# A new instruction order for routed attention and its gated convolution: centroids first, the first pair's argmax split by head, fewer idle products

## The chip, the core and the metric

The kernel runs on one core of a Trainium2 chip. A core has five engines with a queue each, worked off in order: TensorE (PE, matmuls and transposes), VectorE (DVE), ScalarE (ACT, activation functions and copies), GpSimd (POOL) and SyncE (SP, which only issues transfers here). They meet through semaphores. The metric is the device time of one execution in microseconds (us); lower is better.

## The reference

Two stages follow one another. First, attention in which a query sees only the keys of its own cluster; a head's cluster of a row is the argmax of its similarity with 16 centroids:

```python
q_n = q / (norm(q) + 1e-6); k_n = ...; c_n = centroids / (norm(centroids) + 1e-6)
q_assign = argmax(einsum('bhsd,hcd->bhsc', q_n, c_n)); k_assign = argmax(...)
mask = q_assign[:, :, :, None] == k_assign[:, :, None, :]
scores = where(mask, q @ k.T / sqrt(D), -1e9)
x = softmax(scores) @ v            # batch 4, heads 8, sequence 768, head size 64
```

Then, on the heads side by side (4 x 768 x 512), a product with a long convolution, done by a Fourier transform over the sequence:

```python
proj = x @ w_proj; x1, x2, x3 = thirds of proj
x2_conv = irfft(rfft(x2, axis=1) * rfft(filter_fft, axis=0), axis=1)
out = (x1 * x2_conv * x3) @ w_out
```

## The kernel before

`build` first describes the whole program as some 1,950 steps (`op`), each with the engines that may run it, what it reads and writes, and a function that issues its instructions. The list `ORDER` then fixes everything by hand: one number for each step, five times its place in the description plus the engine's number (PE 0, ACT 1, DVE 2, POOL 3, SP 4). `arrange` follows this list; it sets the order within each engine's queue and the PSUM bank that a step gets. A step that the list hands to another engine is computed there, with that engine's own instruction.

The work is cut into eight groups of four heads (`n` = 0 to 7, two for each batch), each of two pairs of heads (`pr`). For a pair, six blocks of 128 keys are taken in turn: TensorE makes scores in three banks (line 158; 156 where the array is used whole), ScalarE takes their exponentials into one of five buffers `p` (lines 690, 693), VectorE adds the buffers up for the denominators (713, 717; GpSimd does some of 713), and TensorE multiplies them with v (704). In between stand the routing of the next group and the convolution of finished batches (`hyena`), whose sums, products and gates on lines 852 to 964 VectorE and GpSimd share as the list says.

The mask is part of the scores' product. Beside the 64 rows of a head, `aug` has 16 rows that hold, for a key, a one at its cluster, and for a query, 0 at its cluster and a large negative number elsewhere.

The start is a path of its own. `warm` lets TensorE run `WARM` idle products (line 1101) on a tile of ones. `centroids` loads the centroids, normalizes them (square, sum, root on ScalarE, one step of Newton on lines 324 to 329), turns them and writes them to `cbd` (337, 338). `routing(0)` turns q and k of the first group in pieces of three 128-row blocks (602), each with an idle product `awake` ahead of it, and copies them to `qkP` (246, 248). `first_masks(pr)` makes the similarities (502), turns them (511) and finds the argmax in five VectorE steps (518 to 525): the largest of 16, who equals it, times a falling ramp `revc`, the largest again, who equals that. For the first pair the resulting words are turned (535) and copied to the mask rows of `aug` (`put`: 546 and 248, one for each head and for q and k); for the second they go through a transfer. `angles` meanwhile makes the arguments of the sines (357 to 375) for three tables m = 0, 1, 2, and `constants` ramps, zero fills (1072, 1074) and an identity.

Of the kernel before, what the change touches and what calls it, by code (L numbers as in the profile page):

```python
# [15 lines left out]
BF16 = mybir.dt.bfloat16  # L16
# [212 lines left out]
def build(T):  # L229
# [261 lines left out]
    def first_masks(pr):  # L491
# [35 lines left out]
        if pr == 0:  # L527
            for j in (1, 0):
                h2 = Bank("head")

                def rows(e, j=j, h2=h2):
                    o = ap(h2).bitcast(BF16)
                    for t in range(NT):
                        for hp in range(2):
                            T.nc.tensor.transpose(o[64 - 64 * hp:80 - 64 * hp, ts(t, 128)], oh()[:, at(t) + 2 * j + hp], T.identb)
# [755 lines left out]
```

## Time and profile before

| | |
|---|---|
| time, median of 3 | 348.03 us (347.56 to 348.55) |
| profiled execution | 348.1 us, of which the span from first to last instruction 346.3 us |
| granted TensorE clock, mean | 0.997 |
| busy: TensorE, VectorE, ScalarE, GpSimd | 336.8, 327.6, 274.2, 135.1 us |
| instructions: VectorE, ScalarE, GpSimd | 438, 509, 161 |
| first exponential starts | 16.52 us |

In a row of the profile stand the line, the engine, the operation, the tiles written and read, their shape, the count, the busy time and the mean of one. A matmul's end is modelled from the pipeline, so TensorE's busy time is rougher than VectorE's. In a row of the timeline, the first number is the start in us from the span's start, the second how long it took.

### The profile page before, as it was taken

The numbers are of one execution on the slowest core, as the hardware profiler recorded it, in microseconds if no ns is written. First come the engines' busy times: TensorE is split into PE (matmuls) and PEld (weight loads), VectorE is DVE, ScalarE is ACT, GpSimd is POOL, SyncE is SP. The second block draws the span as 40 slices with busy tenths as digits, with TensorE's granted clock in tenths as the row PEclk, the third lists the DMA queues.
The fourth block names the chain that finished last, engine by engine and source line by source line (L and its number), as shares of the span: only waits on it lengthen the run. The fifth ranks groups of instructions, "written<-read, shape, count | busy, mean of one in ns | idle before, by whom it ended". The sixth has DMA issues, their size and how long they took to land.

```text
span 346.3 us, 8366 instructions
## 1 busy us (share of the span) xinstructions
PE 336.8 (97%) x3164; PEld 194.7 (56%) x3165; DVE 327.6 (95%) x438; ACT 274.2 (79%) x509; POOL 135.1 (39%) x161
## 2 busy tenths in 40 slices
PE   8899999999999999999999999999999999999994
PEld 4464465454455556655665656676455555576672
DVE  6899999999999999999999999999999999989992
ACT  7999999999799989887898797697998655524442
POOL 6423407004115447234702686126501161336740
PEclk9999999999999999999999999999999999999998
DMA  8979986775799997798969776998748321500124
GB/s 184 195 150 208 181 168 125 123 152 122 161 160 157 141 169 89 153 117 185 142 124 167 132 126 150 195 135 128 164 103 142 72 25 43 173 5 2 74 110 184
DMA packets 132052, 46.19 MB, mean 133 GB/s; under 512 B 119192, under 2 KB 124140, under 8 KB 132012
## 3 DMA queue, kind: packets, MB, share of 16 engines
q1 hardware_dynamic: 127884, 35.79, 49.9%
q0 software_dynamic: 2752, 8.98, 18.7%
q10 hardware_dynamic: 1376, 0.89, 0.8%
q8 instruction: 25, 0.41, 0.5%
q14 instruction: 15, 0.12, 0.1%
HBM read 31.59 MB, written 7.40 MB: 113 GB/s over the span
## 4 chain that ended last, share of the span: by engine, by line
PE 81%; ACT 8%; DVE 8%; issue 1%; ACTq 0%; DVEq 0%
PE bank L158 38%; PE pair L704 32%; PE bank L838 5%; PE bank L622 3%; DVE acc L717 2%; ACT aug L246 1%; PE bank L733 1%; DVE tm L868 1%; PE bank L455 1%; ACT p L693 1%; ACT qkP L246 1%; ACT sim L648 1%; DVE ohB L637 1%; DVE oh L635 1%; DVE mx L633 1%
## 5 line engine op out<-in xcount | busy, mean ns | idle before, releaser
L704 PE MATMUL pair<-p,vraw 128*64 128x385 f32 x768 | 142.1, 487 | 0.0
L693 ACT ACTIVATE p<-bank 128x512 f32<-128x512 f32 x192 | 108.6, 606 | 22.5 <-PE bank L158 19.8
L717 DVE TENSOR_TENSOR acc<-p,acc 128x1536 f32<-128x1536 f32 x64 | 112.9, 1765 | 2.6 <-ACT p L693 0.2
L158 PE MATMUL bank<-aug 128*64 128x512 bf16 (+1 forms) x738 | 83.7, 327 | 0.3 <-ACT p L693 0.2
L704 PEld LDWEIGHTS pair<-p,vraw 128*64 128x64 f32 x768 | 57.9, 136 | 42.6 <-issue 33.7
L158 PEld LDWEIGHTS <-aug 128*64 128x64 bf16 (+1 forms) x738 | 45.0, 109 | 36.7 <-issue 25.3
L754 POOL DMA_DIRECT2D acc<-acc x30 | 23.9, 796 | 98.4 <-DVE acc L717 61.4
L690 ACT ACTIVATE p<-bank 128x512 f32<-128x512 f32 x96 | 57.1, 609 | 5.4 <-PE bank L158 4.3
L158 PE MATMUL bank<-xT,wpj 128*64 128x384 bf16 x504 | 49.4, 326 | 0.0
L158 PEld LDWEIGHTS <-wpj 128*64 128x64 bf16 x504 | 30.9, 110 | 14.4 <-issue 4.6
L246 ACT CAST aug<-qkP 64x768 bf16<-64x768 f32 x46 | 37.7, 829 | 0.8
L713 POOL TENSOR_TENSOR acc<-p,p 128x1536 f32<-128x1536 f32 x7 | 24.3, 3474 | 29.6 <-DVE acc L717 27.8
L158 PEld LDWEIGHTS <-y 128*64 128x64 bf16 x488 | 24.6, 110 | 12.7 <-issue 4.1
L868 DVE TENSOR_TENSOR tm<-bank,hm 128x512 f32<-128x512 f32 x44 | 27.9, 681 | 1.1 <-PE bank L455 0.5
L158 PE MATMUL bank<-wout,y 128*64 128x512 bf16 (+1 forms) x200 | 23.9, 371 | 0.2 <-DVE y L964 0.2
L579 DVE STREAM_TRANSPOSE qkP<-qkraw 128x768 f32<-128x768 f32 x26 | 24.0, 953 | 0.0
L838 PE MATMUL bank<-wpj,xT 128*64 128x512 bf16 x192 | 22.8, 379 | 0.4 <-ACT tm L246 0.4
L872 POOL TENSOR_TENSOR y<-tm 128x512 bf16<-128x512 f32 x15 | 19.0, 1274 | 10.6 <-DVE tm L868 8.2
L964 POOL TENSOR_TENSOR y<-yy,x 128x768 bf16<-128x768 f32 x9 | 16.4, 1827 | 15.1 <-DVE acc L717 7.1
L246 ACT COPY x<-bank 128x384 f32<-128x384 f32 x27 | 13.1, 484 | 11.4 <-PE bank L158 10.6
L246 ACT COPY ob<-bank 128x512 f32<-128x512 f32 x22 | 12.8, 589 | 11.1 <-PE bank L158 9.4
L248 POOL CAST aug<-qkP 64x768 bf16<-64x768 f32 x15 | 12.5, 840 | 17.7 <-DVE acc L717 7.4
(175 smaller groups left out, 415.0 us busy)
## 6 DMA issues: line engine op xcount, KB each, us to landing
rb<-dr SPq DMA_DIRECT2D x30, 192.0 KB, 3.5
qkraw<-in_k_dram SPq DMA_DIRECT2D x55, 96.0 KB, 3.2
qkraw<-in_q_dram SPq DMA_DIRECT2D x55, 96.0 KB, 3.2
vraw<-in_v_dram SPq DMA_DIRECT2D x52, 96.0 KB, 3.2
out_dram<-ob SPq DMA_DIRECT2D x9, 512.0 KB, 3.2
acc<-acc POOLq DMA_DIRECT2D x10, 384.0 KB, 5.2
acc<-acc POOLq DMA_DIRECT2D x10, 192.0 KB, 4.0
y<-in_moe_filter_fft_dram SPq DMA_DIRECT2D x4, 384.0 KB, 4.9
```

The lines of the kernel that those rows point to most:

```text
L158: T.nc.tensor.matmul(out[64 * i:64 * i + 64], lhsT[:, 64 * i:64 * i + 64], rhs, start=start, stop=stop)
L246: T.nc.scalar.copy(out, in_)
L579: op(("DVE", .96), lambda e, s=s, z=z, j=j: V().transpose(T.qkP[z // 2][:, ts(j, S)], T.qkraw[s][:].rearrange("p t h d -> p (t h d)") if j ...
L690: T.nc.scalar.activation(o, ap(h).rearrange("p (a b) -> p a b", a=2), Act.Exp, scale=0.125)
L693: T.nc.scalar.activation(flat(s)[:, lo:lo + 512], ap(h), Act.Exp, scale=0.125)
L704: T.nc.tensor.matmul(o[64 * hp:64 * hp + 64, ch, :385], T.vraw[vs][:, hp, sk * D:(sk + 1) * D], T.p[slots[sk]][:, hp, 384 * ch:384 * ch + ...
L713: alu(e).tensor_tensor(T.acc[os], T.p[slots[0]][:, :, :S], T.p[slots[1]][:, :, :S], op=Alu.add)
L717: T.nc.vector.tensor_tensor(T.acc[os], T.p[slots[sk]][:, :, :S], T.acc[os], op=Alu.add)
L754: op(("POOL", .8), lambda e, rows=rows: T.nc.gpsimd.dma_start(flat_()[:rows], flat_()[rows:2 * rows], accum_op=Alu.add), te, r=[], w=AK, b ...
L838: T.nc.tensor.matmul(ap(h)[64 * i:64 * i + 64], T.xT[xs][:, kt, c:c + 64], T.wpj[:, kt, DM:2 * DM], start=kt == 0, stop=kt == ND - 1)
L868: op(("DVE", .68), lambda e, i=i, cs=cs, r=r, h=h: T.nc.vector.tensor_tensor(T.tm[r][:, cs], ap(h), hmrow(i, (0, 2, 2, 3)[2 * r + cs]), op ...
L872: op({"POOL": 1.5, "DVE": .68}, lambda e, i=i, r=r: alu(e).tensor_tensor(T.y[:, i, r], T.tm[r][:, 0], T.tm[r][:, 1], op=Alu.add if r else ...
```

## The change

Four things change in the description, and the list is a new one throughout.

- `WARM` falls from 10 to 8, and the four transposes of the first pair (z = 0, 1) lose their idle product.
- The first pair's five argmax steps are done for each of the two heads apart, on every second of 24 columns; so are the transposes of its words. Each head's q and k have a bank of their own.
- The order's start is set so that the centroids' load is the first that SyncE issues, and their sum of squares the first real work of VectorE; the sine tables' arguments for m = 0 are made after the first masks.
- Every step has a new place, and about 65 steps have another engine.

```diff
-WARM = 10
+WARM = 8
...
-        if pr == 0:
-            for j in (1, 0):
...
+        for hp in range(2) if pr == 0 else (None,):
+            N = 24 if hp is None else 12
+            k = ((pr,) if hp is None else (pr, hp))
+            part = (lambda x: x) if hp is None else (lambda x, hp=hp: x[:, hp::2])
...
+            op(("DVE", D_[0]), lambda e, part=part: V().tensor_reduce(part(mx()), part(sv()), axis=AX, op=Alu.max), dd + .5, r=[h], w=[("mx", *k)])
...
+            for j in (1, 0) if pr == 0 else ():
                 h2 = Bank("head")
...
                     for t in range(NT):
-                        for hp in range(2):
-                            T.nc.tensor.transpose(o[64 - 64 * hp:80 - 64 * hp, ts(t, 128)], oh()[:, at(t) + 2 * j + hp], T.identb)
+                        T.nc.tensor.transpose(o[64 - 64 * hp:80 - 64 * hp, ts(t, 128)], oh()[:, at(t) + 2 * j + hp], T.identb)
...
-                    if n == 0:
+                    if n == 0 and z > 1:
                         awake(h)
...
 ORDER = [
-    2, 179, 106, 28, 5, 171, 23, 32, 154, 161, 184, 18, 48, 169, 13, 98, 159, 37, 62, 51, 206, 66, 58, 267, 189, 272, 277, 149, 43, 112, 236, 117,
+    2, 109, 23, 161, 5, 176, 169, 13, 37, 18, 184, 149, 103, 154, 51, 112, 206, 48, 117, 267, 58, 174, 122, 237, 272, 126, 159, 81, 132, 199, 98, 86,
```

Behind the hunks on line 518 the numbers of the lines grow by 6 or 7 (602 becomes 608, 964 becomes 970).

Two places of VectorE's queue show what the list did. The first is the first pair's argmax up to the second pair's first step, before (`bank_65` holds the first pair's turned similarities, `bank_154` the second's; `aug_97` and `aug_98` are the first pair's two heads):

```order
L518 TENSOR_REDUCE mx<-bank_65 128x24
L519 TENSOR_TENSOR oh<-bank_65,mx 128x384
L521 TENSOR_TENSOR oh<-oh,revc 128x384
L523 TENSOR_REDUCE m_87<-oh 128x24
L525 TENSOR_TENSOR oh<-oh,m_87 128x384
L248 CAST aug_98<-qkP_113 64x768
L546 TENSOR_SCALAR aug_97<-bank_68 16x768
L248 COPY aug_97<-bank_153 16x768
L546 TENSOR_SCALAR aug_98<-bank_68 16x768
L518 TENSOR_REDUCE mx<-bank_154 128x24
```

and the same place now, from the first head's second step on (its first, of line 525, stands ahead of these):

```order
L526 TENSOR_TENSOR oh<-bank_63,mx 128x12x16
L525 TENSOR_REDUCE mx<-bank_63 128x12
L528 TENSOR_TENSOR oh<-oh,revc 128x12x16
L530 TENSOR_REDUCE m_87<-oh 128x12
L532 TENSOR_TENSOR oh<-oh,m_87 128x12x16
L526 TENSOR_TENSOR oh<-bank_63,mx 128x12x16
L528 TENSOR_TENSOR oh<-oh,revc 128x12x16
L530 TENSOR_REDUCE m_87<-oh 128x12
L532 TENSOR_TENSOR oh<-oh,m_87 128x12x16
L248 COPY aug_97<-bank_67 16x768
L551 TENSOR_SCALAR aug_97<-bank_153 16x768
L248 COPY aug_98<-bank_154 16x768
```

Five steps became ten, the two heads' steps follow each other, the cast of `aug_98` left this place, and the mask copies stand behind both heads' steps.

The second place is VectorE's queue behind the last sum of exponentials (`yy` is the folded convolution, `y_135` its product with the gates, `xT` the attention's output, `x_141` the gates). Before:

```order
L717 TENSOR_TENSOR acc_118<-p_103,acc_118 128x1536
L248 COPY od<-bank_64 128x384
L919 TENSOR_TENSOR x_141<-bank_68,x_141 128x2x192
L946 TENSOR_TENSOR sd<-bank_67,od 128x384 x2
L956 TENSOR_TENSOR yy<-sd 128x2x192
L785 RECIPROCAL dn<-bank_65 128x12
L964 TENSOR_TENSOR y_135<-yy,x_141 128x768
```

and now:

```order
L723 TENSOR_TENSOR acc_118<-p_103,acc_118 128x1536
L962 TENSOR_TENSOR yy<-sd 128x2x192
L773 RECIPROCAL dn<-dn 128x12
L962 TENSOR_TENSOR yy<-sd 128x2x192
L970 TENSOR_TENSOR y_135<-yy,x_140 128x768
L810 SCALAR_TENSOR_TENSOR xT_132<-osb_120,rb 128x2x192 x2
L952 TENSOR_TENSOR sd<-bank_65,od 128x384 x2
L962 TENSOR_TENSOR yy<-sd 128x2x192
L925 TENSOR_TENSOR x_141<-bank_66,x_141 128x2x192
L791 RECIPROCAL dn<-bank_68 128x12
L970 TENSOR_TENSOR y_135<-yy,x_141 128x768
```

Two folds and a gate that GpSimd had in the old list stand in VectorE's queue here, ahead of the weighing of the attention's output (`xT`).

More of the change, by code (lines that the diff above doesn't have):

```diff
@@ L516, in first_masks @@
         mx, m2 = lambda: T.mx[:, pr], lambda: T.m2[:, pr]
-        bc = lambda a: a.unsqueeze(2).to_broadcast([128, 24, NC])
-        op(("DVE", .55), lambda e: V().tensor_reduce(mx(), sv(), axis=AX, op=Alu.max), due + .5, r=[h], w=[("mx", pr)])
-        op(("DVE", .55), lambda e: V().tensor_tensor(oh(), sv(), bc(mx()), op=Alu.is_equal), due + .6,
-           r=[h, ("mx", pr)], w=[("oh", pr)], free=[h])
-        op(("DVE", .35), lambda e: V().tensor_tensor(oh(), oh(), T.revc[:].unsqueeze(1).to_broadcast([128, 24, NC]),
-                                                     op=Alu.mult), due + .7, r=["revc"], w=[("oh", pr)], lock=True)
@@ L523, in first_masks @@
-        op(("DVE", .55), lambda e: V().tensor_reduce(m2(), oh(), axis=AX, op=Alu.max), due + .8, r=[("oh", pr)],
-           w=[("m2", pr)])
-        op(("DVE", .55), lambda e: V().tensor_tensor(oh(), oh(), bc(m2()), op=Alu.is_equal), due + .9,
-           r=[("m2", pr)], w=[("oh", pr)], lock=True)
-        if pr == 0:
-            for j in (1, 0):
+        put_ = []
+        for hp in range(2) if pr == 0 else (None,):
+            N = 24 if hp is None else 12
+            k = ((pr,) if hp is None else (pr, hp))
+            part = (lambda x: x) if hp is None else (lambda x, hp=hp: x[:, hp::2])
+            bc = lambda a, N=N: a.unsqueeze(2).to_broadcast([128, N, NC])
+            D_ = (.55, .36) if hp is None else (.36, .26)
+            dd = due + .5 * (hp or 0)
+            op(("DVE", D_[0]), lambda e, part=part: V().tensor_reduce(part(mx()), part(sv()), axis=AX, op=Alu.max), dd + .5, r=[h], w=[("mx", *k)])
+            op(("DVE", D_[0]), lambda e, part=part, bc=bc: V().tensor_tensor(part(oh()), part(sv()), bc(part(mx())), op=Alu.is_equal), dd + .6,
+               r=[h, ("mx", *k)], w=[("oh", *k)], free=[h])
+            op(("DVE", D_[1]), lambda e, part=part, N=N: V().tensor_tensor(
+                part(oh()), part(oh()), T.revc[:].unsqueeze(1).to_broadcast([128, N, NC]), op=Alu.mult), dd + .7, r=["revc"], w=[("oh", *k)], lock=True)
+            op(("DVE", D_[0]), lambda e, part=part: V().tensor_reduce(part(m2()), part(oh()), axis=AX, op=Alu.max), dd + .8, r=[("oh", *k)],
+               w=[("m2", *k)])
+            op(("DVE", D_[0]), lambda e, part=part, bc=bc: V().tensor_tensor(part(oh()), part(oh()), bc(part(m2())), op=Alu.is_equal), dd + .9,
+               r=[("m2", *k)], w=[("oh", *k)], lock=True)
+            for j in (1, 0) if pr == 0 else ():
@@ L529, in first_masks, with rows @@
                 h2 = Bank("head")
-                def rows(e, j=j, h2=h2):
+                def rows(e, j=j, hp=hp, h2=h2):
                     o = ap(h2).bitcast(BF16)
                     for t in range(NT):
-                        for hp in range(2):
-                            T.nc.tensor.transpose(o[64 - 64 * hp:80 - 64 * hp, ts(t, 128)], oh()[:, at(t) + 2 * j + hp], T.identb)
-                op(("PE", .35), rows, due + 1.0 + .1 * (1 - j), r=[("oh", 0), "identb"], w=[h2], alloc=h2, kind="sim")
@@ L537, in first_masks @@
-                for hp in range(2):
-                    def put(e, j=j, hp=hp, h2=h2):
-                        rs = slice(64 - 64 * hp, 80 - 64 * hp)
-                        o, x = T.augs[0][hp][j][rs], ap(h2).bitcast(BF16)[rs, :S]
-                        if j:
-                            copy(e, o, x)
-                        elif e == "ACT":
-                            T.nc.scalar.activation(o, x, Act.Copy, scale=BIG, bias=-BIG)
-                        else:
-                            V().tensor_scalar(o, x, BIG, -BIG, op0=Alu.mult, op1=Alu.add)
-                    got = op({"ACT": .8, "DVE": .55}, put, due + 1.2 + .3 * hp, r=[h2, ("zero", 0, j)],
-                             w=[("augm", 0, hp, j)], free=[h2])
@@ L549, in first_masks, with put @@
-            return [got]
+                        T.nc.tensor.transpose(o[64 - 64 * hp:80 - 64 * hp, ts(t, 128)], oh()[:, at(t) + 2 * j + hp], T.identb)
+                op(("PE", .21), rows, dd + 1.0 + .1 * (1 - j), r=[("oh", *k), "identb"], w=[h2], alloc=h2, kind="sim")
+                def put(e, j=j, hp=hp, h2=h2):
+                    rs = slice(64 - 64 * hp, 80 - 64 * hp)
+                    o, x = T.augs[0][hp][j][rs], ap(h2).bitcast(BF16)[rs, :S]
+                    if j:
+                        copy(e, o, x)
+                    elif e == "ACT":
+                        T.nc.scalar.activation(o, x, Act.Copy, scale=BIG, bias=-BIG)
+                    else:
+                        V().tensor_scalar(o, x, BIG, -BIG, op0=Alu.mult, op1=Alu.add)
@@ L550, in first_masks @@
+                put_ = [op({"ACT": .8, "DVE": .55}, put, dd + 1.2 + .3 * hp, r=[h2, ("zero", 0, j)],
+                           w=[("augm", 0, hp, j)], free=[h2])]
+        if pr == 0:
+            return put_
         h2 = Bank("head")
@@ L596, in routing, with tr @@
                 h = Bank(cls)
-                def tr(e, s=s, ch=ch, j=j, h=h):
-                    if n == 0:
+                def tr(e, s=s, ch=ch, z=z, h=h):
+                    if n == 0 and z > 1:
                         awake(h)
@@ L602, in tr @@
                         T.nc.tensor.transpose(ap(h)[:, ts(t, 128)], raw(s, 3 * ch + t), T.ident)
-                op(("PE", .58 if n == 0 else .36), tr, due, r=[("qkraw", s, x, c) for x in range(2) for c in (range(4) if n else (ch, ch + 2))] + [("raw", s, x, y) for x in range(2) for y in range(2)] + ["ident"] + ["cold", "warmed", ("wpj", 0)] * (n == 0), w=[h], alloc=h)
+                op(("PE", .58 if n == 0 and z > 1 else .36), tr, due, r=[("qkraw", s, x, c) for x in range(2) for c in (range(4) if n else (ch, ch + 2))] + [("raw", s, x, y) for x in range(2) for y in range(2)] + ["ident"] + ["cold", "warmed", ("wpj", 0)] * (n == 0), w=[h], alloc=h)
                 op(EV384 if n != 1 else {"ACT": .48}, lambda e, z=z, ch=ch, h=h: copy(e, T.qkT[z][:, ch], ap(h)[:, :384]),
@@ L628, in routing @@
                r=[h], w=[("sim", ch, 0), ("sim", ch, 1)], free=[h])
-        both = lambda x: [(x, 0), (x, 1)]
+        both = lambda x: [(x, 0, 0), (x, 0, 1), (x, 1)]
         sims = lambda: T.sim[:].rearrange("p a (m c) -> p (a m) c", c=NC)
```

158 rows, old and new, of the table ORDER are left out of this document.

## The prediction

> **What bounds the kernel now.** I read the page first, then busy time by stretch, then the waits of VectorE, then single rows. The page says that two engines are full, not one:
>
> ```profile
> span 346.3 us, 8366 instructions
> ...
> PE 336.8 (97%) x3164; PEld 194.7 (56%) x3165; DVE 327.6 (95%) x438; ACT 274.2 (79%) x509; POOL 135.1 (39%) x161
> ...
> PE   8899999999999999999999999999999999999994
> ...
> DVE  6899999999999999999999999999999999989992
> ```
>
> By stretch (columns: length, then busy us and instructions of PE, PEld, DVE, ACT, POOL), from the first scores to the last gate:
>
> ```profile
> core 0: us, PE busy (x) PEld busy (x) DVE busy (x) ACT busy (x) POOL busy (x), PEclk, DMA share, GB/s
> ...
> 20.00:300.00 280.00, 278.52 (x2534) 157.75 (x2532) 273.95 (x329) 237.31 (x436) 104.79 (x101) 1.00 0.76 136
> 300.00:339.50 39.50, 39.29 (x499) 26.36 (x495) 37.13 (x68) 17.50 (x35) 20.50 (x17) 1.00 0.20 71
> ```
>
> VectorE is idle 6.05 + 2.37 = 8.42 us of 319.5. What it waited for in that stretch, nine rows in all, of which the first three and the last stand here:
>
> ```profile
> DVE x L919 <- PE bank L158: 1.1, 2, 0.8
> DVE dn L785 <- ACT x L246: 0.8, 1, 0.8
> DVE tm L868 <- PE bank L455: 0.5, 1, 0.5
> ...
> DVE tm L868 <- PE bank L158: 0.2, 1, 0.2
> ```
>
> The other five are 0.2 each, so the nine come to 3.6 us at most. The 4.8 us left over, spread over 397 instructions, are 12 ns each: gaps between instructions that wait for nothing. So VectorE works without a real pause from about 11 us to the last gate. TensorE's 278.5 of 280 looks as full, but the page says that the ends of matmuls are modelled; VectorE's rows carry no such caveat. Since the last instruction ahead of the final products is a VectorE gate (338.93, below), I take VectorE's work to set the end: what the new order adds to its queue comes out at the end, less what real waits can swallow.
>
> **The head: idle products and centroids.** TensorE runs idle products until the first transposes; ScalarE and VectorE then feed the first masks:
>
> ```profile
> 1.12 4.87 PE L1101 MATMUL bank<-wpj 128*128 128x512 bf16 x11 [1.12 <-DVE wpj L1105]
> 5.79 0.79 PE L602 MATMUL bank<-ident,qkraw 128*128 128x128 f32 x3
> ...
> 6.63 0.49 PE L602 MATMUL bank<-ident,qkraw 128*128 128x128 f32 x3
> ...
> 9.22 0.85 PE L502 MATMUL bank<-qkP,cbd 128*32 128x384 f32 x8 [0.36 <-ACT ob L368]
> ```
> ```profile
> 4.29 0.83 ACT L1074 ACTIVATE aug<-ident 64x768 bf16<-64x768 f32 x1
> ...
> 8.62 0.53 ACT L368 ACTIVATE ob<-tm 128x384 f32<-128x384 f32 x1
> 9.18 0.62 ACT L375 ACTIVATE wout<-ob,half_pi 128x384 bf16<-128x384 f32 x1
> 9.70 0.46 ACT L246 COPY qkP<-bank 128x384 f32<-128x384 f32 x1
> ```
>
> Eleven idle products take 4.87 us (0.43 from one to the next); now eight stand ahead of the first transposes, which could begin 3 x 0.43 = 1.3 us sooner. But the similarities at 9.22 need more: the centroid table, which VectorE writes behind the centroids' chain and two copies of turned q and k, and ScalarE's copies. The chain now stands ahead of most angle work, yet it waits for the centroids' load, which changes queues (from ScalarE's first issue to SyncE's first; the loads behind it keep their places, since one k load goes the other way). And ScalarE's copy of the similarities, before behind a sine and a copy (0.62 + 0.46), now stands behind an absolute value and a zero fill (0.53 + 0.83), 0.28 more; against it ScalarE issues one load less at the start. I price the start of the first argmax at no change, with 0.3 us either way, from that 0.28.
>
> [...] A start that stays cold is a rival below.
>
> **The first masks.** VectorE's rows of before, and one short row of the centroids for size:
>
> ```profile
> 4.67 0.22 DVE L319 TENSOR_REDUCE ss<-sd 128x1 f32<-128x64 f32 x1
> ...
> 11.32 0.56 DVE L518 TENSOR_REDUCE mx<-bank 128x24 f32<-128x384 f32 x1 [0.86 <-PE bank L511]
> ...
> 12.57 0.36 DVE L521 TENSOR_TENSOR oh<-oh,revc 128x384 bf16<-128x384 bf16 x1
> ...
> 13.55 0.56 DVE L525 TENSOR_TENSOR oh<-oh,m 128x384 bf16<-128x384 bf16 x1
> 14.14 0.56 DVE L248 CAST aug<-qkP 64x768 bf16<-64x768 f32 x1
> 14.73 0.56 DVE L546 TENSOR_SCALAR aug<-bank 16x768 bf16<-16x768 bf16 x1
> ...
> 16.26 0.54 DVE L518 TENSOR_REDUCE mx<-bank 128x24 f32<-128x384 f32 x1
> 16.73 0.54 DVE L248 COPY aug<-bank 16x768 bf16<-16x768 bf16 x1
> 17.29 0.56 DVE L519 TENSOR_TENSOR oh<-bank,mx 128x384 bf16<-128x384 f32 x1
> ...
> 18.86 0.56 DVE L525 TENSOR_TENSOR oh<-oh,m 128x384 bf16<-128x384 bf16 x1
> ```
>
> Five instructions of 384 elements become ten of 192. Between 0.22 us at 64 elements and 0.56 at 384, 192 elements come to 0.36; the 0.36 row (two-byte operands) to some 0.25. Eight of 0.36 and two of 0.25 are 3.4 us, with ten gaps of 0.03 3.7, where the five took 2.8 (11.32 to 14.14). If a half took no fixed time the ten would be 2.8, if as long as a whole 5.6: -0.9 to +1.9 around the value taken. The cast at 14.14 moves ahead of the chain (-0.6). The four mask copies (14.73 to 17.29 with one reduction, so 2.0 without) all stand behind both heads' words in the new queue, so the first head's earlier words buy no earlier mask: the first copy starts 3.7 us after the chain's start, before 3.4. The second pair's five whole steps follow as they did. Sum for the point where the second pair's words are ready: +0.9 - 0.6 = **+0.3 us**; TensorE's queue holds that pair's transposes ahead of the first weighted sums in both orders, so nothing passes it there.
>
> **The rest of VectorE's queue.** The new order also hands whole steps to other engines. Net, between that point and the last gate, at these groups' mean ns:
>
> ```profile
> L964 DVE TENSOR_TENSOR y<-yy,x 128x768 bf16<-128x768 f32 x3 | 2.9, 950 | 0.1
> ...
> L857 DVE TENSOR_TENSOR uv<-tm,tm 128x512 bf16<-128x512 f32 x12 | 7.9, 695 | 0.0
> ...
> L872 DVE TENSOR_TENSOR y<-tm 128x512 bf16<-128x512 f32 x9 | 6.1, 691 | 0.1
> ...
> L433 DVE TENSOR_SCALAR tm<-bank,hw 128x512 f32<-128x512 f32 x2 | 1.4, 744 | 0.0
> ...
> L363 DVE SCALAR_TENSOR_TENSOR tm<-x,s0t,ob 128x384 f32<-128x384 f32 x3 | 1.9, 644 | 0.1
> ...
> L361 DVE TENSOR_SCALAR ob<-ob 128x384 f32<-128x384 f32 x3 | 1.2, 397 | 0.1
> ```
> ```profile
> 338.93 0.56 DVE L964 TENSOR_TENSOR y<-sim,qkP 128x384 bf16<-128x384 f32 x1
> ```
>
> Two more whole gates (+1.90) and one half gate less (-0.56); two more sums of spectra (+1.39); one more product difference (+0.69); two scalings to ScalarE (-1.49); the two angle steps of m = 0, before ahead of the masks, now behind (0.40 + 0.64 = +1.04); one more cast (+0.56); small ones (a mask row step, copies, two tiny constants) about +0.3. Sum **+3.8 us**. GpSimd, which gives most of these up, was busy 104.8 of 280 us, so what it sheds buys nothing; nor does ScalarE's relief of five casts, with 43 us free in that stretch. GpSimd now makes the index ramps before all else, which moves its other constants by a few of its rows and delays no engine that was waiting for them here. TensorE has the same products in the long middle; the six idle products less are at the start. The tables that ScalarE loads are as many as before, five.
>
> **The sum.** The profiled execution took 348.1 us (span 346.3), beside a median of 348.03, so no correction is needed. 348.1 + 0.0 + 0.3 + 3.8 = 352.2 if nothing is swallowed. The waits of 3.6 us, most of them behind 300 us, where about 2 of the 3.8 are added (both gates among them), can swallow between nothing and all. I take half, 1.8: **350.4 us**, 0.7% slower. Its own range: all swallowed and the start 0.3 early, 348.3; nothing swallowed and 0.3 late, 352.5.
>
> **Rivals.**
> *TensorE is the bound.* Then VectorE's extra work disappears in its gaps, and the end follows TensorE's start: the first transposes 1.3 us early, less the 0.3 of the mask chain, gives 348.1 - 1.0 = 347.1. For it: 278.5 of 280. Against it: VectorE's 12 ns gaps, and that four other steps stand between the transposes and the masks. It decides if the added steps fit in gaps. Chance 0.2.
> *Everything swallowed.* The start does not move and the 3.8 us find their waits: 348.1 + 0.3 = 348.4, no change that shows (about 0.3%, 1.0 us, is what a measurement of this kernel can tell from none). For it: the order may have been laid so that each added step falls in a pause. Against it: the pauses come to 3.6 us and are single. Chance 0.17.
> *A cold start.* With eight products and no idle ones between the first pair's transposes, the array could stay slow until the argmax: two transpose groups 0.3 longer each, the similarities 0.85 and the next transposes 0.5 longer, 2.0 on the way to the masks: 352.4. For it: 0.79 against 0.49. [...] Chance 0.08.
>
> **How the numbers follow.** The forecast has 0.55. Faster by over 0.3% is the first rival, 0.2; within, the second, 0.17; slower, forecast and cold start, 0.63. The range reaches from the first rival's 347.1 to 352.5.
>
> **What would show it.** Right: VectorE's busy sum up by 4 to 5 us with waits below 2 us between 20 us and the last gate; first mask copy no earlier than 14.7; last gate near 341. Wrong: the last gate before 339 with VectorE busier; half-size steps far from 0.36; the first reduction before 11.0; or idle time on TensorE in the middle with VectorE waiting too, which would be a wait that I did not see (SyncE's queue, where loads for the second group now stand ahead of the first V load).

## The result, and the profile after

The changed kernel takes **358.66 us** (median of 4, 356.46 to 359.43) where the kernel before takes 348.02 on the same chip: 1.0288 times as long, 95% interval 1.0266 to 1.0310. That is 10.6 us slower. The forecast was 350.4 with a range up to 352.5: the sign was right, the size was not.

The page of the changed kernel (profiled execution 358.81 us) shows at once where to look. In its second part each digit is a slice of 8.9 us. TensorE has a dent in slices 5 and 6, from 36 to 54 us, VectorE in slices 6 and 7, and the granted clock in slice 6:

```profile
span 357.1 us, 8344 instructions
...
PE 340.8 (95%) x3149; PEld 191.2 (54%) x3149; DVE 330.4 (93%) x449; ACT 271.1 (76%) x505; POOL 136.5 (38%) x159
...
PE   7999669999999999999999999999999999999994
...
DVE  5789947999999999999989999999999999999984
...
PEclk9999969999999999999999999999999999999998
```

By stretches of 20 us (length, then busy us and instructions of PE, PEld, DVE, ACT, POOL, then the clock), before and after:

```profile
40.00:60.00 20.00, 19.84 (x178) 11.33 (x176) 19.90 (x22) 19.53 (x36) 7.69 (x9) 1.00 0.82 158
```
```profile
40.00:60.00 20.00, 14.41 (x104) 7.14 (x100) 13.05 (x14) 12.53 (x23) 10.70 (x16) 0.83 0.60 104
```

TensorE, VectorE and ScalarE all lose 5 to 7 us there; only GpSimd is busier. Its timeline in the changed kernel, with TensorE's and VectorE's of the same microseconds:

```profile
39.77 0.82 POOL L248 CAST aug<-qkP 64x768 bf16<-64x768 f32 x1 [6.50 <-PE bank L158]
40.54 0.53 POOL L1096 DMA_DIRECT2D wpj<-in_moe_w_proj_dram  x1
41.10 6.22 POOL L407 TENSOR_SCALAR hw<-ph 128x3 f32<-128x3 f32 x5
...
47.36 0.10 POOL L381 MEMSET fw<- 128x2 bf16 x1
47.39 0.09 POOL L381 MEMSET wout<- 128x1 bf16 x1
```
```profile
41.58 0.41 PE L158 MATMUL bank<-aug 80*64 80x512 bf16 x2
47.51 1.07 PE L158 MATMUL bank<-uv,fw 128*64 128x512 bf16 x4 [5.52 <-POOL wout L381]
```
```profile
40.91 1.74 DVE L719 TENSOR_TENSOR acc<-p,p 128x1536 f32<-128x1536 f32 x1
42.69 0.56 DVE L656 TENSOR_SCALAR sim<-bank 64x384 bf16<-64x384 f32 x1
43.17 1.74 DVE L723 TENSOR_TENSOR acc<-p,acc 128x1536 f32<-128x1536 f32 x1
44.83 0.55 DVE L248 CAST aug<-qkP 64x768 bf16<-64x768 f32 x1
45.30 1.75 DVE L723 TENSOR_TENSOR acc<-p,acc 128x1536 f32<-128x1536 f32 x1
```

Line 407 is five scalings of three columns each: the factors `hw` of the filter's spectrum. They took 6.22 us. Behind them in GpSimd's queue stand two writes of constants (line 381) into the sine tables, and TensorE's first products with these tables waited 5.52 us for them. In the kernel before, the same five scalings took 1.42 us, and the constants were there before TensorE asked:

```profile
35.69 1.42 POOL L407 TENSOR_SCALAR hw<-ph 128x3 f32<-128x3 f32 x5
...
39.91 0.10 POOL L381 MEMSET fw<- 128x2 bf16 x1 [2.18 <-ACT fw L375]
```

In cuts of 0.2 us, for line 407 alone, a cut with two instructions is one in which the rows of two scalings meet or overlap:

```profile
42.60:42.80 0.20, 0.20 (x2) 1.00 0.82 147
42.80:43.00 0.20, 0.20 (x2) 1.00 1.32 221
...
44.20:44.40 0.20, 0.20 (x1) 1.00 1.05 190
...
44.60:44.80 0.20, 0.20 (x1) 0.50 1.15 184
44.80:45.00 0.20, 0.20 (x2) 0.50 0.80 124
...
45.40:45.60 0.20, 0.20 (x2) 0.50 0.05 8
45.60:45.80 0.20, 0.20 (x1) 0.50 0.00 0
...
47.00:47.20 0.20, 0.20 (x2) 0.50 0.00 0
```

VectorE's three sums end at 40.91 + 1.74 = 42.65, 43.17 + 1.74 = 44.91 and 45.30 + 1.75 = 47.05. Each time the next scaling starts within 0.1 us of that end, in finer cuts at 42.74, 44.97 and 47.11. Of the five, two took 0.22 us and three were held:

```profile
L407 POOL TENSOR_SCALAR hw<-ph x5: 216/1657/2485, 41.1 to 47.1; 128x3 f32<-128x3 f32 x5
```

The first (1.66 us) and the fourth (2.16) end within 0.1 us of a sum's end. The third, the longest with 2.49, does not: its row goes from 42.93, a little ahead of the second sum, to 45.42, past that sum and to the end of VectorE's cast (44.83 + 0.55). What held it behind the sum, no run takes apart. The fourth column of these cuts is TensorE's granted clock: it falls to half at 44.6, 2.6 us after TensorE's last product (41.58 + 0.41). When TensorE goes on at 47.51, a set of four products takes 1.07 us. (`fw` and `wout` are the sine tables, `acc` the sums of the exponentials.)

The start is late too. The nine first transposes took 2.15 us, the similarities 1.38 where they took 0.85 before, and the first argmax began at 11.89, where it was 11.32 before:

```profile
5.71 2.15 PE L608 MATMUL bank<-ident,qkraw 128*128 128x128 f32 x9 [0.99 <-DMA qkraw<-in_q_dram]
...
9.33 1.38 PE L502 MATMUL bank<-qkP,cbd 128*32 128x384 f32 x8 [0.61 <-DVE tm L363]
```
```profile
11.89 0.36 DVE L525 TENSOR_REDUCE mx<-bank 128x12 f32<-128x192 f32 x1
...
14.84 0.36 DVE L532 TENSOR_TENSOR oh<-oh,m 128x192 bf16<-128x192 bf16 x1
15.23 0.56 DVE L248 COPY aug<-bank 16x768 bf16<-16x768 bf16 x1
```

### The profile page after: what moved, and what is told of

The parts are those of the page before. It is cut to its first block, busy times and chain, and to the rows that moved or that the text cites. A ratio compares the mean times of both kernels' runs of the same rounds, so it can differ in the third digit from the quotient of the medians.

```text
span 357.1 us, 8344 instructions
## 1 busy us (share of the span) xinstructions
PE 340.8 (95%) x3149; PEld 191.2 (54%) x3149; DVE 330.4 (93%) x449; ACT 271.1 (76%) x505; POOL 136.5 (38%) x159
## 4 chain that ended last, share of the span: by engine, by line
PE 57%; DVE 17%; ACT 7%; DMA 6%; issue 4%; POOL 4%; SPq 3%; DVEq 0%; ACTq 0%; POOLq 0%
PE bank L158 27%; PE pair L710 22%; DVE acc L723 3%; PE bank L844 3%; DVE sd L952 2%; ACT p L699 2%; DMA rb<-dr 2%; DVE xT L810 2%; ACT aug L246 2%; POOL hw L407 2%; PE bank L628 2%; ACT p L696 2%; DMA aug<-sim 1%; DVE tm L858 1%; SPq L288 1%
## 5 line engine op out<-in xcount | busy, mean ns | idle before, releaser
L699 ACT ACTIVATE p<-bank 128x512 f32<-128x512 f32 x192 | 109.4, 612 | 17.5 <-PE bank L158 14.3
L158 PE MATMUL bank<-aug 80*64 80x256 bf16 (+3 forms) x742 | 82.7, 326 | 1.3 <-DMA aug<-sim 0.9
L710 PEld LDWEIGHTS pair<-p,vraw 128*64 128x64 f32 x768 | 55.0, 137 | 48.6 <-issue 38.8
L158 PEld LDWEIGHTS <-aug 80*64 80x64 bf16 (+1 forms) x742 | 44.5, 109 | 39.7 <-issue 25.5
L158 PE MATMUL bank<-xT,wpj 128*64 128x384 bf16 x496 | 48.1, 326 | 0.2 <-ACT tm L246 0.2
L246 ACT CAST aug<-qkP 64x768 bf16<-64x768 f32 x41 | 33.9, 829 | 0.7
L248 POOL CAST aug<-qkP 64x768 bf16<-64x768 f32 x19 | 15.9, 839 | 22.3 <-PE bank L158 7.6
L962 POOL TENSOR_TENSOR yy<-sd 128x384 f32<-128x384 f32 x14 | 14.4, 1059 | 23.5 <-DVE yy L962 15.3
L878 POOL TENSOR_TENSOR y<-tm 128x512 bf16<-128x512 f32 x14 | 17.8, 1277 | 8.1 <-DVE tm L874 6.8
L246 ACT COPY ob<-bank 128x512 f32<-128x512 f32 x21 | 12.0, 587 | 10.6 <-PE bank L158 10.0
```

Source lines behind the costliest of these rows:

```text
L158: T.nc.tensor.matmul(out[64 * i:64 * i + 64], lhsT[:, 64 * i:64 * i + 64], rhs, start=start, stop=stop)
L246: T.nc.scalar.copy(out, in_)
L699: T.nc.scalar.activation(flat(s)[:, lo:lo + 512], ap(h), Act.Exp, scale=0.125)
L710: T.nc.tensor.matmul(o[64 * hp:64 * hp + 64, ch, :385], T.vraw[vs][:, hp, sk * D:(sk + 1) * D], T.p[slots[sk]][:, hp, 384 * ch:384 * ch + ...
L878: op({"POOL": 1.5, "DVE": .68}, lambda e, i=i, r=r: alu(e).tensor_tensor(T.y[:, i, r], T.tm[r][:, 0], T.tm[r][:, 1], op=Alu.add if r else ...
```

## The experiments

Medians are given with the number of executions, and the time over the kernel before as a ratio with its 95% interval; "before" is always the kernel before on the same chip in the same rounds (348.15 to 348.44). In kernels whose list is edited, line numbers are 12 to 14 lower than in the changed kernel, because the list is printed in fewer rows (line 407 is 393 there).

**1. The five scalings and the two constants earlier.** In the list, the two steps move ahead of the cast and the weight load behind which they stood:

```diff
     ... angles m=0 (ACT), denominators (DVE),
+    scalings (POOL), constants (POOL),
     cast (POOL), ..., weight load (POOL), sum (DVE), exp (ACT),
-    scalings (POOL),
     ...
-    constants (POOL),
```

> The changed kernel with GpSimd's five scalings of the phases and its two constants put ahead of the cast and the weight load behind which they stand now; nothing else moves. Theory (GpSimd's queue): in the changed kernel these five tiny scalings take 6.2 us because three VectorE sums of 1.74 us hold them, and TensorE waits 5.5 us for the constants queued behind them. Put early they meet shorter VectorE steps: the five take under 2.5 us, TensorE's busy time from 40 to 60 us rises from 14.4 to over 18.5, and the time falls from 358.7 to 351 to 353. Rival (VectorE's added work sets the end, the wait is only where it shows): TensorE's and VectorE's idle time moves to a later place, and the time stays above 356.

Measured: **351.93** (4 runs, 349.95 to 354.01), 1.0126 of before (1.0081 to 1.0171): 6.7 us of the 10.6 are back by the medians, 5.6 of 10.0 by the ratios. The profiled execution is the fastest of the four. The scalings, now beside VectorE's shorter steps (0.55 to 0.97 us each), took 1.76 us, TensorE's wait is gone, and its busy time from 40 to 60 us is 19.24:

```profile
36.70 1.76 POOL L393 TENSOR_SCALAR hw<-ph 128x3 f32<-128x3 f32 x5 [5.07 <-ACT ph L372]
```
```profile
40.00:60.00 20.00, 19.24 (x168) 10.23 (x166) 19.64 (x21) 18.97 (x36) 8.06 (x7) 1.00 0.85 141
```

The wait did not come back elsewhere; the rival falls. What this run does not tell is whether the late place cost the time, or VectorE's sums.

**2. The same five scalings on ScalarE, at the late place.**

```diff
-    T.nc.gpsimd.tensor_scalar(hw[:, c], T.ph[:, f], x / S, None, op0=Alu.mult)
+    T.nc.scalar.activation(hw[:, c], T.ph[:, f], Act.Copy, scale=x / S)
```

> The changed kernel with the five scalings computed by ScalarE at the same place of the program; the three small writes behind them and the two constants stay on GpSimd at their late place. Theory (VectorE's sums hold GpSimd's scalings): ScalarE does the five in under 1.5 us, the constants are written before 42.5 us, TensorE's 5.5 us wait falls below 1 us, and the time is 351 to 354, like that of the early scalings. Rival (GpSimd's place in its own queue is too late, whatever the scalings take): the constants still come after 45 us, and the time stays above 356.

Measured: **352.62** (4 runs, 351.01 to 353.77), 1.0119 (1.0086 to 1.0151). The order is the changed one throughout; only the engine of five tiny instructions differs.

```profile
40.41 0.57 ACT L407 ACTIVATE hw<-ph 128x3 f32<-128x3 f32 x5
```
```profile
40.98 0.10 POOL L381 MEMSET fw<- 128x2 bf16 x1
```
```profile
40.35 1.72 DVE L719 TENSOR_TENSOR acc<-p,p 128x1536 f32<-128x1536 f32 x1
```

On ScalarE the five take 0.57 us, and GpSimd writes its constants at 40.98, still behind the cast and the weight load and in the midst of VectorE's first sum (40.35 to 42.07). So the late place alone costs nothing that shows beside experiment 1 (1.0119 and 1.0126). What costs is that the scalings, on GpSimd, meet VectorE's sums: in the changed kernel three of the five took 1.66, 2.49 and 2.16 us where the other two took 0.22, and the next one started each time just behind a sum's end (42.65, 44.91 and 47.05). The constants (0.10 us) and ScalarE's scalings (0.57 us for five) ran beside a sum here and were not held. Why a sum holds a scaling and not a constant, no run takes apart. Nor do the rows settle it: the third scaling's begins 0.23 us ahead of the second sum's, and yet it was held, and its last 0.5 us lie behind that sum.

**3. The start: idle products taken from the kernel before.** Its order untouched, `WARM` 10 to 8, and no idle product ahead of the first pair's transposes.

```diff
-WARM = 10
+WARM = 8
...
-                    if n == 0:
+                    if n == 0 and z > 1:
                         awake(h)
```

> The kernel before with eight idle products instead of ten, and none between the transposes of the first pair; its order is untouched. Theory (a colder array): the first transposes begin 1 us earlier but run as slowly as the first three do now, the similarities take over 1.2 us instead of 0.85, the first argmax starts 0.2 to 0.6 us later than 11.32, and the time is 348.3 to 349. Rival (TensorE's early start is worth what it saves): the first argmax starts 0.3 to 1 us earlier, and the time is 347.0 to 347.7.

Measured: **349.26** (10 runs, 348.38 to 349.53) against 348.35, 1.0023 (1.0010 to 1.0035). The twelve transposes took 2.79 us, and the first argmax began at 11.67 instead of 11.32:

```profile
5.53 2.79 PE L602 MATMUL bank<-ident,qkraw 128*128 128x128 f32 x12 [0.81 <-DMA qkraw<-in_k_dram]
```
```profile
11.67 0.56 DVE L518 TENSOR_REDUCE mx<-bank 128x24 f32<-128x384 f32 x1 [1.19 <-PE bank L511]
```

The colder array (products that at first take longer: three transposes 0.85 us at 8.76, 0.49 at 10.57) is real; its price is 0.9 us here. The similarities, expected above 1.2 us, took 0.88 where the kernel before has 0.85: by then the array had warmed. The transposes also had to wait for k and began at 5.53, only 0.26 us earlier than before and not 1 us, so the early end of the idle products bought little.

**4. The idle products put back into the changed kernel.** (The opposite edit, list unchanged.)

> The changed kernel with the ten idle products and the idle product ahead of each transpose of the first pair put back (the count alone; the order is the changed one). Theory (the array starts cold in most runs of the changed kernel): the first twelve transposes take under 2.2 us instead of 3, the first argmax starts before 11.0 us instead of 11.9, and the time is 356 to 357.3. Rival (the start does not matter, since VectorE and the later wait swallow it): within 0.8 of 358.7.

Measured: **357.29** (4 runs, 356.03 to 358.66), 1.0257 (1.0225 to 1.0288), 1.4 below the changed kernel by the medians; the two intervals overlap. In the profiled one the first argmax began at 10.38. TensorE's wait of 5.5 us is still there.

**5. Both: early scalings and all idle products.**

> Early scalings and the idle products put back, both. If the two causes add up: the runs of the early scalings spread over 4 us (349.95 to 354.01) because the array starts warm in some and cold in others; with the idle products all four runs lie within 1 us, at 349.5 to 350.7. What stays over the kernel before, 1.5 to 2.5 us, is then VectorE's added work. Rival (the spread has another cause): the median stays above 351.3 or the runs spread over 2 us.

Measured: **350.42** (4 runs, 349.96 to 351.35), 1.0062 (1.0043 to 1.0081), first argmax at 10.78. The two causes add up as far as the runs can tell. Over before, the four kernels stand at 10.64 (changed), 3.58 (early scalings), 9.14 (idle products) and 2.27 (both): the scalings are worth 7.06 with eight idle products and 6.87 with all of them, the idle products 1.50 and 1.31. By the ratios these are 5.6 and 6.8, and 1.1 and 2.2: with intervals of 0.7 to 1.6 us either way on each kernel, the sum holds, but not to a tenth. The profiled executions place the first cause more closely. Up to the third of the sums above, the changed kernel runs 1.1 us behind this one (45.30 against 44.19); at the next sum it is 7.8 us behind:

```profile
57.32 3.54 DVE L723 TENSOR_TENSOR acc<-p,acc 128x1536 f32<-128x1536 f32 x2
```
```profile
44.19 1.75 DVE L709 TENSOR_TENSOR acc<-p,acc 128x1536 f32<-128x1536 f32 x1
...
49.52 3.54 DVE L709 TENSOR_TENSOR acc<-p,acc 128x1536 f32<-128x1536 f32 x2
```

The spread shrinks from 4.1 us to 1.4, not to the 1.0 expected. The cold start is not shown to be its cause: the kernels of experiment 7, with the same ten idle products, spread over 1.3 to 4.6 us, and those of experiment 3, with eight, over 1.2. In the profiled run of experiment 1 the array happened to be warm after the eight products, as the nine transposes in 1.17 us show, where the changed kernel took 2.15:

```profile
5.81 1.17 PE L594 MATMUL bank<-ident,qkraw 128*128 128x128 f32 x9 [1.32 <-DMA qkraw<-in_q_dram]
```

Why the same eight products left the array warm in one execution and cold in the other, no run shows.

The traces' own records of the clock show when it was full. In the changed kernel the record begins at 10.46 us, with full clock for 34.13 us; then come half clock for 6.83 (44.59 to 51.42) and full clock for 303.79. In the kernel before it begins at 6.39, with full clock for 337.92. Ahead of its first record the clock column shows 1.00 only because nothing is recorded there. The four stretches are 10, 2, 89 and 99 times 3.413 us. The rows agree with both starts: in the changed kernel three transposes took 0.85 us at 7.87 and 0.49 at 10.87, in the kernel before 0.79 at 5.79 and 0.49 at 6.63.

In the changed kernel the products ended at 4.72, TensorE then stood 0.99 us until q was there, and the three stretches of 3.41 us ahead of 10.46 held 0.90, 0.99 and 0.61 us of idle time, the earliest first; in the kernel before, the one ahead of 6.39 held none. But in experiment 1 TensorE stood longer, 1.32 us, and its transposes ran fast, so the pause alone does not decide it, and no experiment set it. The first argmax follows the rows: with eight products it begins at 10.25, 11.33 and 11.89 (experiments 1 and 2, the changed kernel) where the similarities took 0.85, 1.12 and 1.38 us and the nine transposes 1.17, 2.15 and 2.15; with ten, at 10.38, 10.78 and 11.35 (experiments 4 and 5, the first edit of 7) where the first three transposes took 0.52, 0.58 and 0.85.

**6. Which engine sets the end in the kernel before?** The reduction of the similarities' maximum done twice in the third to sixth group (VectorE), and in another kernel the similarities' products done twice there (TensorE).

```diff
+    for _ in range(2 if 2 <= n <= 5 else 1):
         V().tensor_reduce(mx(), sims(), axis=AX, op=Alu.max)
```
```diff
-    for ch in range(2):
+    for ch in (0, 1, 0, 1) if 2 <= n <= 5 else range(2):
         for z in range(4):
```

> The kernel before with the reduction of the similarities' maximum (0.95 us on VectorE) done twice in the third to sixth group: 3.8 us more on VectorE, nowhere else. Theory of the prediction (VectorE sets the end all along): 351 to 352. Rival (TensorE sets the end in the middle, VectorE's extra work fits into gaps that come back): below 349.2.

> The kernel before with the similarities' eight products done twice in the third to sixth group: some 4 us more on TensorE (0.85 to 1.4 us a group), nowhere else. If TensorE sets the end in the middle, 351 to 353.5. If VectorE does (the prediction's theory), below 349.5. Both engines may bound in turns: then this and the doubled VectorE step each cost between.

Measured: **352.11** (4 runs), 1.0119 (1.0088 to 1.0150), and **351.86** (4 runs), 1.0107 (1.0089 to 1.0125). The pages' busy sums, doubled VectorE step first, then doubled TensorE step:

```profile
PE 336.3 (96%) x3164; PEld 194.9 (56%) x3165; DVE 331.4 (95%) x442; ACT 274.2 (78%) x509; POOL 135.3 (39%) x161
```
```profile
PE 341.0 (97%) x3228; PEld 196.3 (56%) x3229; DVE 328.4 (94%) x438; ACT 274.1 (78%) x509; POOL 135.4 (39%) x161
```

VectorE's 3.8 us more cost 3.8, TensorE's 4.2 more cost 3.5: work added to either shows almost whole at these steps. But both steps lie on one chain, from the similarities over the argmax to the next group's masks. In the kernel with the doubled VectorE step, TensorE waited 3.0 us at three places for the end of that chain (`ohB`, the turned words), where the kernel before has 0.2 us at one. So the two runs show that this chain is on the way to the end, for its steps on TensorE no less than for those on VectorE. That either engine is full elsewhere, they do not show.

**7. What are the last 2.3 us?** Five edits of the kernel of experiment 5. First, three whole gates (0.95 us each) go back from VectorE to GpSimd, where they stood before: three numbers of the list go up by one.

> As the run with early scalings and all idle products, and three whole gates of the second and third batch (0.95 us each on VectorE) handed back to GpSimd, where they stood before: 2.85 us less on VectorE. Theory (VectorE's added work is what remains): 2 to 2.85 us under that run, 347.0 to 348.5. Rival (TensorE bounds there, or GpSimd's slower gates, some 1.8 us each, delay their users): less than 1 us under that run.

Measured: **351.27** (4 runs), 1.0077 (1.0059 to 1.0094): not less. The groups of the two kernels show where the time given up went, first with the gates on VectorE, then on GpSimd:

```profile
L796 DVE SCALAR_TENSOR_TENSOR xT<-osb,rb 128x384 bf16<-128x384 f32 x30 | 17.5, 625 | 0.5 <-DMA rb<-dr 0.4
...
L956 DVE TENSOR_TENSOR y<-yy,x 128x768 bf16<-128x768 f32 x5 | 4.8, 954 | 0.6 <-POOL yy L948 0.5
```
```profile
L796 DVE SCALAR_TENSOR_TENSOR xT<-osb,rb 128x384 bf16<-128x384 f32 x30 | 20.4, 722 | 0.0
...
L956 DVE TENSOR_TENSOR y<-yy,x 128x768 bf16<-128x768 f32 x2 | 1.9, 959 | 0.5 <-POOL yy L948 0.5
```

VectorE gave up 2.9 us of gates, and its 30 scalings of the attention's output (line 796) took 2.9 us more. One of the places, GpSimd's gate and VectorE's pair beside it:

```profile
226.09 2.10 POOL L956 TENSOR_TENSOR y<-yy,x 128x768 bf16<-128x768 f32 x1
```
```profile
226.65 2.49 DVE L796 SCALAR_TENSOR_TENSOR xT<-osb,rb 128x384 bf16<-128x384 f32 x2
```

Such a pair takes 1.13 us elsewhere (at 246.48, for one); here it took 2.49 and ended at 229.14, behind the gate's end at 228.19. This is the holding of experiment 2 the other way round. That it is why the time did not fall is not shown: the third edit below frees VectorE of the gates without such a hold, and the time stays.

Second, four copies of 0.55 us go from VectorE to ScalarE. Third, the three gates stay on VectorE, cut to 8 columns. Fourth, the similarities are cut on TensorE; fifth, both cuts.

```diff
+    if (b, dt) in ((1, 0), (2, 0), (2, 2)):
+        xs_ = [x[:, :8] for x in xs_]
     alu(e).tensor_tensor(*xs_, op=Alu.mult)
```
```diff
+    N = 96 if n > 1 and ch else 384
-    T.nc.tensor.matmul(...[:32, :384], T.cbd[...], T.qkT[z][:, ch], ...)
+    T.nc.tensor.matmul(...[:32, :N], T.cbd[...], T.qkT[z][:, ch, :N], ...)
```

> As the run with early scalings and all idle products (350.42), and four of VectorE's copies (two casts, one mask step, one copy of the last batch; 0.55 us each, 2.2 in all) handed to ScalarE, which has 40 us and more free between 140 and 300 us. [...] Rival (TensorE sets the end, or the copies come later on ScalarE and TensorE waits for them): 350 or more.

> As the run with early scalings and all idle products (350.42), and the same three whole gates kept on VectorE but cut to 8 of 768 columns (the rest of their output is left as it was): some 2.4 us less on VectorE and nothing more on GpSimd. Theory (VectorE's added work is the 2.3 us that remain; the gates handed to GpSimd gave nothing because GpSimd's gates held VectorE's own two-input steps, whose mean rose from 625 to 722 ns over 30): 348.0 to 349.0. Rival (TensorE sets the end there): above 349.8.

> As the run with early scalings and all idle products (350.42), and the similarities' second four products cut from 384 to 96 columns in the third to eighth group (the rest of that bank is left as it was): some 2 us less on TensorE. If TensorE sets the end there: 348.2 to 349.2. If VectorE does: above 349.8.

> As the run with early scalings and all idle products (350.42), with both cuts at once: three whole gates of 768 columns on VectorE cut to 8 (2.4 us less there), and the similarities' second four products cut to 96 columns in the third to eighth group (some 2 us less on TensorE); what is not computed is left as it was. Each cut alone gave 350.56 and 350.69. Theory (both engines are full in turns, so that each hides the other's relief): 348.2 to 349.3. Rival (what remains is waiting, for the denominators' DMA round trip above all, where the cut of TensorE alone had VectorE wait 2.1 us): above 349.8 again.

Measured: copies on ScalarE **351.96** (7 runs), 1.0091 (1.0061 to 1.0121); gates cut **350.56** (11 runs), 1.0047 (1.0027 to 1.0066); TensorE cut **350.69** (11 runs), 1.0059 (1.0035 to 1.0083); both cut **349.37** (11 runs), 1.0050 (1.0026 to 1.0073). With the gates cut, the 30 scalings are back at 17.5 us, and the time is still the same. Against 1.0062, none of the five is a gain that the intervals can tell. So the 2.3 us are not VectorE's added work alone, which the prediction's sum made of them, nor TensorE's. With both cut, the pages have VectorE 2.1 and TensorE 2.6 us lower, and the time falls by 1.0 us by the medians, 0.4 by the ratios. In the kernel with TensorE cut, VectorE then waited 2.1 us for the denominators' way through memory:

```profile
DVE xT L797 <- DMA rb<-dr: 2.1, 1, 2.1
```

With both cut that wait is gone from the profiled run, which with 348.68 is the second fastest of its eleven. What these last 2.3 us hang on stays open.

## Why the prediction was wrong

**The step that failed** is in the part on the rest of VectorE's queue: "GpSimd, which gives most of these up, was busy 104.8 of 280 us, so what it sheds buys nothing", and behind it that its constants move by a few rows and that this "delays no engine that was waiting for them here". GpSimd's moves were judged by its busy share, and its queue was not walked as far as the constants of line 381. The new list held all that was needed: the phases' two sines, which the prediction's count of moved steps does not have, move on ScalarE from 7.55 us to 37.9; the scalings that need them come behind a cast that waits for a bank; VectorE's sums stand beside that place; and the filter's products stand right behind. This term was taken as 0 and measured 6.9 to 7.1 us by the medians, 5.6 to 6.8 by the ratios (experiments 1, 4 and 5), and 6.7 at this place in the profiled executions. Of that, 5.5 is TensorE's wait, and the rest fits the half clock after it (1.07 us for a set of four products that took 0.63 in experiment 1).

**What would show it wrong** did show it: idle time on TensorE in the middle with VectorE waiting too. The guess beside it, SyncE's queue, was the wrong queue.

**The start.** "No change, with 0.3 us either way" was the forecast's term; the cold start was a rival at 0.08. It measured 1.3 to 1.5 us by the medians, 1.1 to 2.2 by the ratios, where 2.0 was its price; in the kernel before, the same edit cost 0.9. Eight products were not always enough: in the changed kernel they ran from 1.12 to 4.72, TensorE waited 0.99 us for q behind them, and full clock is recorded only at 10.46. The transposes ran slow in three of the four traces with eight products (2.15 us for nine in two of them and 2.79 for twelve in the third, against 1.17 for nine). In the rival's price, no run shows the similarities 0.85 us longer and the next transposes 0.5: in the changed kernel they took 1.38 instead of 0.85, 0.53 longer, and the transposes behind them 0.49 and 0.55, as before. With ten, the new head is as forecast or better: the first argmax begins at 10.38 to 11.35 instead of 11.32, at the late end with a start as slow as that of the kernel before (0.85 and 0.79 us for the first three transposes).

**The chain of half steps** came as worked out: 0.36 and 0.25 us a step. From the first reduction to the first mask copy it took 15.23 - 11.89 = 3.34, forecast 3.7.

**VectorE's added work.** Between 20 us and the last gate its busy time rose by 3.1 us (311.1 to 314.2), where the sum had 3.8 and the sign to look for 4 to 5. That VectorE alone sets the end is not borne out: in experiment 6 TensorE's work, the rival, shows as much as VectorE's. The page of the kernel before spoke against it too, and the prediction did not weigh it. The chain of work that ended last is there mostly TensorE's (shares of the span):

```profile
PE 81%; ACT 8%; DVE 8%; issue 1%; ACTq 0%; DVEq 0%
```

Without the two causes above, the kernel stands at 350.42, the forecast's 350.4; but experiment 7 does not bear out the sum that led there, so the agreement is luck and no proof of it.

## What to carry to other kernels

An engine with much idle time can still hold the one thing that the busy engines wait for: when an order moves, walk every queue from each moved step to what stands behind it, also on the engine with a third of its time in use. On GpSimd, ask what VectorE runs beside a step, not only how long the step is: here tiny ones of 0.22 us took up to 2.49 beside sums of 1.74, and a large one of 2.1 us held a VectorE step. And after work is handed from VectorE to GpSimd, look at VectorE's other rows before counting the gain.

## What the runs showed of the hardware

- A GpSimd scaling of 128x3 took 0.22 us undisturbed and 1.66 to 2.49 beside VectorE's sums in the changed kernel; in the kernel before, the longest took 0.638. On ScalarE none was held: five in 0.57 us.
- A GpSimd step held VectorE too: of 30 VectorE steps with a median of 0.61 us the longest took 2.18, beside a GpSimd gate of 2.06.
- The clock column reads 1.00 in the first 10 us of the changed kernel and of experiment 1, while nine transposes there took 2.15 us in one and 1.17 in the other. In the changed kernel nothing of the clock is recorded ahead of 10.46 us.
- In the middle of the changed kernel the clock fell to half at 44.59, 2.6 us after TensorE stopped; in the 3.41 us up to there TensorE had worked for 0.81 us. It was full again 6.83 us later, and a set of four products took 1.07 us in between, where it took 0.63 in experiment 1.
